# One tile of a seven-product block multiplication moved behind the next product, with its operand work reordered

## The chip, the cores and the metric

The kernel runs on one core of a Trainium2 chip. The metric is the device time of one execution in microseconds. TensorE multiplies, VectorE, ScalarE and GpSimd prepare its operands (VectorE and ScalarE also empty its result banks), and SyncE issues the transfers.

## The reference

Attention over clusters, then a layer with a squared ReLU, then the layer that matters here: four experts, each a hidden product, a ReLU and an output product, added up with each token's weight.

```python
def _moe2_ref(x, domain_probs, w1, w2):     # x 1536x512, w1 4x512x1024, w2 4x1024x512
    p = domain_probs / (domain_probs.sum(-1, keepdims=True) + 1e-09)
    out = np.zeros((N, D), dtype=np.float32)
    for e in range(E):
        h = np.maximum(x @ w1[e], 0.0)
        out += p[:, e:e + 1] * (h @ w2[e])
    return out.astype(np.float32)
```

## The kernel before

The tokens come in two batches of 768. A batch goes through 16 groups (NFQ), one for each 256 hidden columns of an expert; groups 16 to 31 are those of batch 1. All operands are split in a high and a low part, and each product is three matmuls (high x high, high x low, low x high) for each 128 of the contraction.

For batch 1 both matrix products of an expert are made in seven block products instead of eight (a Strassen-Winograd scheme: products 1 to 7, with sums of blocks as operands). `first_product(n, i)` is block product i of the hidden layer for group n: six matmuls of 384 columns. `second_product(m, i)` is block product i of the output layer for a pair of groups, a "half" of an expert, m = 0 to 7: three token tiles (j = 0, 1, 2), each six matmuls of 256 columns. The same function issues one eviction on VectorE for each tile (line 1859 or 1861), which scales the result and adds it to the output. The result banks are accumulated in turn: products 1, 6, 7 and 4 go into banks 5, 6 and 7, products 5 and 3 into banks 2, 3 and 1, and each needs that the eviction of the one before has read its bank. Product 2 uses bank 4 for tiles 0 and 2 (its two halves) and bank 0 for tile 1.

The order is written out by hand, and each engine executes its instructions in that order. The list `seq` in the loop over m interleaves the second products of half m (m1, m5, ...) with first products of later groups (3p and 4p are the rest of the group before; 1a to 4a and 1b to 7b are the two groups of half m + 2). Behind each entry, tables name operand work for half m + 1 (`SECOND`, `NEXT`; `LATE` for m = 6 and `LAST` for m = 7) or m + 2 (`SAME`); `FIRST` does so for the stretch ahead of the loop, with groups and products as keys: (17, 4) is behind product 4 of group 17. The work is named by letter and product:

- H and y make the high part of the hidden and the weight operand (ScalarE, lines 1798, 1800 and 1767);
- L and z make the low part: L on VectorE (lines 1805, 1808; a final g puts it on GpSimd), z on GpSimd (line 1770);
- S is a sum of hidden blocks on VectorE (S5 line 1785, S3 line 1788, S6 line 1794, S7 line 1792 on GpSimd with g), t a sum of weight blocks on GpSimd (line 1764);
- R is a ReLU on ScalarE (line 1781), and N a load of the next weights.

A high part comes ahead of its low part, a sum ahead of both. S5 feeds H5, t6 feeds y6. `first_product` copies product 1, 5 and 6 out with ScalarE (lines 1816, 1818, 1820), product 4 with a ReLU on ScalarE (1822), and adds products 2, 7 and 3 with VectorE (1827); product 7 accumulates on product 6's bank and so needs that product 6 was copied, product 4 likewise needs the addition of product 7.

In front of `FIRST` stands group 16 with the last token tiles of batch 0; `prep` is the weight work of group 17 (ScalarE, GpSimd).

Of the kernel before, what the change touches and what calls it, by code (L numbers as in the profile page):

```python
# [34 lines left out]
def moe_attention_kernel(  # L35
# [59 lines left out]
    NFQ = E * NQ  # L95
# [118 lines left out]
    with tc.manual_schedule():  # L214
# [808 lines left out]
        def product(n, i):  # L1023
            b, first = PROD[i][2:]
            block_product(n % 2, i, pb[n, b][:, 0:HALF], lambda x: r_op(R_OF[i], x, n // NFQ), first)
# [392 lines left out]
        def conv_in(c):  # L1418

            b = 2 * (c % 2)  # L1420
            p, q = [split64(c // 2, 0, b + m, lambda shp, m=m: cv_p[m](shp),
                            (nc.vector, nc.gpsimd)[m and c != 4]) for m in range(2)]

            def a():
                return [a_t[c // 2, 0, b + m]["a"] for m in range(2)]
            return p, q, [lambda: w_sums(a(), *([nc.vector] if c == 4 else []))], [
                [lambda m=m: w_mixed(c % 2, m, a(), nc.gpsimd)] for m in range(2)]
# [63 lines left out]
        p, q, sums2, mix = conv_in(2)  # L1491
# [9 lines left out]
        for c in range(2, NC1 - 1):  # L1501
            p, q, sums2, mix = conv_in(c + 1)
# [130 lines left out]
        def last_relu(n):  # L1633
            h_hi(n, 0, 1)
            h_lo(n, 0, 1)
            swapped(n, 3, nc.vector)
# [63 lines left out]
        def back(n, parts=KEPT):  # L1700

            if n >= 2 * NFQ:
                return
            p = (n % 2) * 1024
            for t, a, b in parts:
                for x in range(2):
                    o = 2048 * (t == "Y") + x * 1024
                    nc.sync.dma_start(
                        out=W[t][x][:, p + a * 256:p + b * 256].bitcast(F32),
                        in_=kept[n - NFQ][:, o + a * 256:o + b * 256])  # L1710
# [7 lines left out]
        def hx(m, r, q):  # L1718

            if m % 2:  # L1720
                return x2_t[r][:, q, 0:S].rearrange("p (f t) -> p f t", f=2)
            return fa8[:, ((0, 3), (2, 5))[r][q]:][:, 0:((2, 2), (5, 3))[r][q]:((1, 1), (4, 2))[r][q]]
# [12 lines left out]
        def h_op(i, x):  # L1735
            t, o = H_AT[i]
            return t[:, o + x * NR:o + (x + 1) * NR].rearrange("p (f t) -> p f t", f=2)

        def y_op(i, x):
            t, o = Y_AT[i][x]  # L1740
            return t[:, o:o + 512].rearrange("p (f d) -> p f d", f=2)
# [68 lines left out]
        def first_product(n, i):  # L1810

            m, q = divmod(n - NFQ, 2)
            product(n, i)
            a, b, c = [pb[n, z][:, 0:HALF] for z in "ABC"]
            if i == 1:
                nc.scalar.copy(hx(m, 0, q)[:, 0], a)
            elif i == 5:
                nc.scalar.copy(hx(m, 1, q)[:, 1], c)
            elif i == 6:
                nc.scalar.copy(hx(m, 1, q)[:, 0], a)  # L1820
            elif i == 4:
                nc.scalar.activation(hx(m, 0, q)[:, 1], a, AF.Relu)
                if n != NFQ + 1:
                    back(n + 2)
            else:
                o, z = {2: (hx(m, 0, q)[:, 0], b), 7: (hx(m, 1, q)[:, 1], a), 3: (hx(m, 1, q)[:, 0], c)}[i]
                nc.vector.tensor_tensor(o, z, o, op=ALU.add)  # L1827
            if n == NFQ + 1:
                back(n + 2, [W_AT[i]])

        def acc_half(t, d):
            if t < 4:
                return x2_t[t // 2][:, t % 2, S + 256 * d:S + 256 * d + 256]
            return x2_t[t - 4][:, d, S + 512:2 * S]

        BLOCK = {1: (0, 0), 5: (1, 1), 6: (0, 1), 2: (0, 0), 7: (1, 1), 3: (0, 1), 4: (1, 0)}

        def second_product(m, i):

            e = m // (NQ // 2)  # L1840
            last = m == NFQ // 2 - 1
            r, d = BLOCK[i]
            b = PROD[i][2]
            for j in range(3):
                o = {"A": bank[5 + j][:, 0:256], "C": bank[(2, 3, 1)[j]][:, 0:256],
                     "B": bank[(4, 0, 4)[j]][:, 256 * (j == 2):][:, 0:256]}[b]
                js = slice(j * 128, (j + 1) * 128)
                for f in range(2):
                    hh, hl = [h_op(i, z)[:, f, js] for z in range(2)]
                    wh, wl = [y_op(i, z)[:, f] for z in range(2)]  # L1850
                    for z, (a, w) in enumerate(((hh, wh), (hh, wl), (hl, wh))):
                        nc.tensor.matmul(  # L1852
                            o, a, w, start=(i in (1, 5, 2) and f == 0 and z == 0),
                            stop=(f == 1 and z == 2), skip_group_check=True)
                t = 3 * r + j
                pc = pe_p[:, NTT + t, e:e + 1]
                acc = acc_half(t, d)
                if m == 0 and i in (1, 5, 6, 4):
                    nc.vector.tensor_scalar(acc, o, pc, None, op0=ALU.mult)
                else:  # L1860
                    nc.vector.scalar_tensor_tensor(  # L1861
                        out=acc, in0=o, scalar=pc, in1=acc, op0=ALU.mult, op1=ALU.add)
                if last and i in (2, 7, 3, 4):
                    nc.sync.dma_start(out=ov[1, t][:, 256 * d:256 * d + 256], in_=acc)
# [7 lines left out]
        def steps(m, ws):  # L1872
            for w in ws.split():
                FS[w[0]](m, int(w[1]), *([nc.gpsimd] if w[2:] else []))

        NM = NFQ // 2
        SECOND = {"m1": "H1 y1 z1 t5 t7", "4b": "S5", "m5": "L1 H5", "m6": "S6 y5 z5 t6",
                  "m2": "H2 H6 y6 y2 z6 z2 t4", "m7": "H7", "m3": "y7 y3 z7 z3", "m4": "H4 y4 z4"}
        NEXT = {"5a": "L5", "6a": "L6", "7a": "L2", "1b": "S3", "3a": "H3 L7", "4a": "N1",
                "5b": "L3", "6b": "L4"}  # L1880
        SAME = {"7a": "R0", "6b": "R1", "2b": "S7g"}
        LATE = dict(SECOND, m2=SECOND["m2"] + " L5", m3=SECOND["m3"] + " L6", m4="H4 y4 z4 L7g")
        LAST = {"m1": "L2 S3", "m5": "H3 L3g", "m6": "L4"}
        FIRST = {(17, 1): "y5 z5 t6", (17, 5): "R1", (17, 2): "y6 y2 z6 z2 t4 S7g", (17, 4): "S5 H1 L1",
                 (18, 5): "H5 S6", (18, 6): "L5 y7 y3 H6 z7 z3", (18, 2): "L6", (18, 7): "H2 y4 z4 L2",
                 (19, 1): "S3 H7 L7g", (18, 4): "H3 H4 N1", (19, 5): "L3", (19, 6): "L4"}

        for n in range(2 * NFQ):
            pb[n, "A"] = bank[n % 2]
# [9 lines left out]
        third(NFQ - 1)  # L1899
        last_relu(NFQ - 1)  # L1900
        first_product(NFQ, 5)
        for f in prep[0:2]:
            f()
        for i in (6, 2, 7):
            first_product(NFQ, i)
        for t in range(NTT):
            token_tile(NFQ - 1, t)
# [8 lines left out]
        for n, i in [(1, 1), (1, 5), (1, 6), (1, 2), (1, 7), (2, 1), (1, 3), (1, 4), (2, 5), (2, 6), (2, 2),  # L1916
                     (2, 7), (3, 1), (2, 3), (2, 4), (3, 5), (3, 6), (3, 2), (3, 7)]:
            first_product(NFQ + n, i)
            steps(0, FIRST.get((16 + n, i), ""))
            ev = "%d%s" % (i, " ab"[n - 1])  # L1920
            if n > 1:
                steps(1, SAME.get(ev, ""))
        for m in range(NM):
            a, b = NFQ + 2 * m + 4, NFQ + 2 * m + 5
            seq = "m1 3p 4p m5 m6 m2 m7 m3 1a m4 5a 6a 2a 7a 1b 3a 4a 5b 6b 2b 7b".split()
            if m + 2 >= NM:
                seq = [x for x in seq if x[1] not in "ab" and (x[1] != "p" or m + 2 == NM)]
            for ev in seq:
                if ev[0] == "m":
                    second_product(m, int(ev[1]))  # L1930
                else:
                    first_product({"p": a - 1, "a": a, "b": b}[ev[1]], int(ev[0]))
                ev = ev.replace("p", "b") if ev in ("3p", "4p") else ev + "_" if ev in ("3b", "4b") else ev
                if m + 2 < NM:
                    steps(m + 1, SECOND.get(ev, ""))
                    steps(m + 1, NEXT.get(ev, ""))
                    steps(m + 2, SAME.get(ev, ""))
                elif m + 2 == NM:
                    steps(m + 1, LATE.get(ev, ""))
                else:  # L1940
                    steps(m, LAST.get(ev, ""))
        mctx.close()
# [30 lines left out]
```

## Time and profile before

| | us |
|---|---|
| median of 3 runs (lowest, highest) | 1016.64 (1015.82, 1018.12) |
| the profiled execution | 1016.12 |
| its span, first to last instruction | 1014.3 |
| TensorE busy in it | 991.1 (98%) |
| VectorE, ScalarE, GpSimd busy | 787.6, 576.2, 609.6 |

Matmuls are pipelined, so that busy time says only that TensorE seldom stands still. The stretch of the hidden products of batch 1 begins at about 743 us, the loop over m at 785.6, and the last matmul is issued at 1010.7.

### The profile page before, as it was taken

The page shows a single profiled execution, that of the slowest core. Times are in us where ns is not written, and L with a number is a line of the kernel's source. Part 1 is how long each engine was busy: PE and PEld are TensorE (multiplying, and loading weights), DVE is VectorE, ACT ScalarE, POOL GpSimd, SP SyncE. Part 2 cuts the span into 40 slices and gives each one's busy share as a digit, 9 for nine tenths or more (in the row PEclk, how much of TensorE's full clock was granted, in tenths as well). Part 3 has the DMA queues.
Part 4 walks back from the last instruction along what each step waited for, and adds up shares of the span by engine and source line. Part 5 has one row for each costly group of instructions (what it writes and reads, how often), then busy time and mean ns, then how long its engine had stood idle before and what let it go on. Part 6 is the DMA issues. An engine that isn't in the chain of part 4 may idle for free.

```text
span 1014.3 us, 16370 instructions
## 1 busy us (share of the span) xinstructions
PE 991.1 (98%) x5889; PEld 906.0 (89%) x5889; DVE 787.6 (78%) x1209; ACT 576.2 (57%) x1139; POOL 609.6 (60%) x589
## 2 busy tenths in 40 slices
PE   8999999999999999999999999999998999999997
PEld 8999999999888888888898998998988999999997
DVE  7898999898799997797675555577666778777786
ACT  7888888987645564445643434444445444544441
POOL 7458777753326604436666676686697654556644
PEclk9999999999999999999999999999999999999999
DMA  7577887761112212221034645545537245533411
GB/s 186 128 165 177 193 187 161 176 157 39 45 40 83 84 42 84 84 82 43 21 126 165 216 177 178 208 156 207 187 118 249 91 167 187 175 121 111 156 42 63
DMA packets 92504, 133.78 MB, mean 132 GB/s; under 512 B 29876, under 2 KB 55368, under 8 KB 92424
## 3 DMA queue, kind: packets, MB, share of 16 engines
q1 hardware_dynamic: 92424, 132.74, 43.6%
q8 instruction: 46, 0.75, 0.3%
q14 instruction: 34, 0.28, 0.1%
HBM read 80.93 MB, written 28.88 MB: 108 GB/s over the span
## 4 chain that ended last, share of the span: by engine, by line
PE 83%; DVE 7%; POOL 4%; DMA 2%; issue 2%; ACT 1%; SPq 0%; DVEq 0%; POOLq 0%; ACTq 0%
PE bank L900 23%; PE bank L931 12%; PE bank L1062 11%; PE bank L1852 8%; PE s L656 6%; PE t L689 6%; PE bank L878 5%; PE po L703 3%; PE po L705 3%; DVE x L1861 2%; DMA raw<-in_moe_w_dram 2%; DVE xa L1808 1%; PE s L878 1%; PE m L478 1%; PE m L393 1%
## 5 line engine op out<-in xcount | busy, mean ns | idle before, releaser
L695 DVE TENSOR_TENSOR ptl<-t,pth 128x384 fp32r<-128x384 f32 x192 | 98.2, 550 | 19.9 <-ACT pth L694 19.3
L900 PE MATMUL bank<-xa,wxh 128*128 128x384 f32 (+1 forms) x392 | 103.8, 345 | 0.5 <-DVE x L1827 0.5
L1861 DVE SCALAR_TENSOR_TENSOR x<-bank,pe_p,x 128x256 f32<-128x256 f32 x156 | 72.8, 480 | 35.2 <-PE bank L1852 34.4
L665 DVE TENSOR_REDUCE nb<-s 128x1 f32<-128x768 f32 x96 | 91.1, 950 | 7.9 <-PE s L656 7.5
L1078 DVE SCALAR_TENSOR_TENSOR x<-bank,pe_p,x 128x512 f32<-128x512 f32 x90 | 67.6, 751 | 35.8 <-PE bank L1062 35.7
L1006 POOL TENSOR_TENSOR wxl<-raw,wxh 128x512 fp32r<-128x512 f32 (+1 forms) x36 | 47.1, 1328 | 70.1 <-ACT wxh L1005 70.1
L694 ACT CAST pth<-t 128x384 fp32r<-128x384 f32 x192 | 84.0, 487 | 9.0 <-PE t L689 8.2
L900 PE MATMUL bank<-xa,wyh 128*128 128x384 f32 (+1 forms) x344 | 88.7, 338 | 0.0
L676 ACT ACTIVATE p<-s,nb 128x768 f32<-128x768 f32 x96 | 88.1, 918 | 0.3 <-DVE nb L665 0.2
L656 PE MATMUL s<-k,q 80*128 80x384 f32 (+1 forms) x384 | 86.2, 345 | 0.1
L689 PE MATMUL t<-identf,p 128*128 128x128 f32 x576 | 85.4, 276 | 0.4 <-DVE ptl L695 0.3
L703 PE MATMUL po<-pth,vv 128*128 128x256 f32 x288 | 80.4, 309 | 0.0
L931 PE MATMUL bank<-gb,wzh 128*128 128x512 f32 x240 | 78.0, 391 | 0.2
L689 PEld LDWEIGHTS t<-identf,p 128*128 128x128 f32 x576 | 67.6, 140 | 9.5 <-DVE ptl L695 6.8
L900 PEld LDWEIGHTS bank<-xa,wxh 128*128 128x128 f32 x392 | 71.4, 188 | 5.2 <-DVE x L1827 0.8
L900 PE MATMUL bank<-rt,wyh 128*128 128x384 f32 (+1 forms) x264 | 71.4, 351 | 3.8 <-ACT x L1820 3.4
L705 PE MATMUL po<-ptl,vv 128*128 128x256 f32 x288 | 72.5, 281 | 0.0
L900 PE MATMUL bank<-xa,wxl 128*128 128x384 f32 (+1 forms) x196 | 67.7, 345 | 0.0
L207 ACT CAST wyh<-raw 128x512 fp32r<-128x512 f32 x36 | 22.3, 622 | 78.1 <-POOL raw L200 60.7
L1770 POOL TENSOR_TENSOR wzl<-raw,wzh 128x512 fp32r<-128x512 f32 x32 | 49.9, 1562 | 26.9 <-ACT wzh L1767 26.9
L656 PEld LDWEIGHTS s<-k,q 80*128 80x128 f32 (+1 forms) x384 | 63.4, 189 | 0.6 <-ACT p L676 0.2
L900 PEld LDWEIGHTS bank<-xa,wyh 128*128 128x128 f32 x344 | 62.0, 188 | 1.4
(354 smaller groups left out, 2980.5 us busy)
## 6 DMA issues: line engine op xcount, KB each, us to landing
raw<-in_moe_w_dram SPq DMA_DIRECT2D x34, 512.0 KB, 4.6
raw<-in_moe_w_dram SPq DMA_DIRECT2D x8, 1024.0 KB, 7.6
raw<-in_moe_w_in_dram SPq DMA_DIRECT2D x7, 1024.0 KB, 5.3
kept<-wyh SPq DMA_DIRECT2D x14, 512.0 KB
kept<-wyl SPq DMA_DIRECT2D x14, 512.0 KB, 2.7
wyh<-kept SPq DMA_DIRECT2D x13, 512.0 KB, 4.6
wyl<-kept SPq DMA_DIRECT2D x13, 512.0 KB, 6.1
raw<-in_moe_w_out_dram SPq DMA_DIRECT2D x6, 1024.0 KB
```

The lines of the kernel that those rows point to most:

```text
L656: nc.tensor.matmul(s[:, j, 0:HALF], stk[i, nq][:, t * 128:(t + 1) * 128], stk[i, nk][:, j * HALF:(j + 1) * HALF], start=first, stop=not first)
L665: nc.vector.tensor_reduce(out=nb, in_=s_ps[u][:, :, 0:HALF], axis=AX.XY, op=ALU.max, negate=True)
L676: nc.scalar.activation(p, s_ps.pop(u)[:, :, 0:HALF], AF.Exp, bias=nb_t.pop(u), accum_out=sums_t[hp][:, i % 2, t:t + 1])
L689: nc.tensor.transpose(tp[:, j], p_sb[u][:, half, j * 128:(j + 1) * 128], identf)
L694: return (lambda: nc.scalar.copy(dh, tp), lambda: nc.vector.tensor_tensor(dl, tp, dh.bitcast(F32), op=ALU.subtract))
L695: lambda: nc.vector.tensor_tensor(dl, tp, dh.bitcast(F32), op=ALU.subtract))
L703: nc.tensor.matmul(po_t[pr], vt[i][:, kt], pth[:, kt], start=(kt == 0), stop=False)
L705: nc.tensor.matmul(po_t[pr], vt[i][:, kt], ptl[:, kt], start=False, stop=(kt == NTT - 1))
L900: nc.tensor.matmul(ps, w[:, ks], x(xx)[:, kt], start=(first and kt == 0 and z == 0), stop=(kt == 1 and z == 2), skip_group_check=True)
L931: nc.tensor.matmul(o, a[:, d], b, start=(ft == 0 and z == 0), stop=(ft == 1 and z == 2))
L1062: nc.tensor.matmul(o, a, w[:, f, cols], start=(f == 0 and z == 0), stop=(f == 1 and z == 2))
L1861: nc.vector.scalar_tensor_tensor(out=acc, in0=o, scalar=pc, in1=acc, op0=ALU.mult, op1=ALU.add)
```

## The change

Product 2 of the output layer is issued as two tiles (event m2) and, behind product 7, one (event m2c). The operand work is spread anew over the events: S5 goes from behind 4p to behind product 5, L1 and H5 from product 5 to product 6, S6 from product 6 to product 7; H2, y2, z2 and t4 follow the third tile, and H6 product 3. L5, L6 and L4 go one product back in the last two halves. In the stretch ahead of the loop S7 of half 0 goes from GpSimd to VectorE, H3 and L3 go to later products of group 19. In group 16, product 6 comes ahead of the weight work.

```diff
-        def second_product(m, i):
+        def second_product(m, i, js=range(3)):
...
-            for j in range(3):
+            for j in js:
...
-        SECOND = {"m1": "H1 y1 z1 t5 t7", "4b": "S5", "m5": "L1 H5", "m6": "S6 y5 z5 t6",
-                  "m2": "H2 H6 y6 y2 z6 z2 t4", "m7": "H7", "m3": "y7 y3 z7 z3", "m4": "H4 y4 z4"}
+        SECOND = {"m1": "H1 y1 z1 t5 t7", "m5": "S5", "m6": "L1 H5 y5 z5 t6", "m2": "y6 z6",
+                  "m7": "S6 H7", "m2c": "H2 y2 z2 t4", "m3": "H6 y7 y3 z7 z3", "m4": "H4 y4 z4"}
...
-        LATE = dict(SECOND, m2=SECOND["m2"] + " L5", m3=SECOND["m3"] + " L6", m4="H4 y4 z4 L7g")
-        LAST = {"m1": "L2 S3", "m5": "H3 L3g", "m6": "L4"}
-        FIRST = {(17, 1): "y5 z5 t6", (17, 5): "R1", (17, 2): "y6 y2 z6 z2 t4 S7g", (17, 4): "S5 H1 L1",
+        LATE = dict(SECOND, m3=SECOND["m3"] + " L5", m4="H4 y4 z4 L6 L7g")
+        LAST = {"m1": "L2 S3", "m5": "H3 L3g", "m7": "L4"}
+        FIRST = {(17, 1): "y5 z5 t6", (17, 5): "R1", (17, 2): "y6 y2 z6 z2 t4 S7", (17, 4): "S5 H1 L1",
                  (18, 5): "H5 S6", (18, 6): "L5 y7 y3 H6 z7 z3", (18, 2): "L6", (18, 7): "H2 y4 z4 L2",
-                 (19, 1): "S3 H7 L7g", (18, 4): "H3 H4 N1", (19, 5): "L3", (19, 6): "L4"}
+                 (19, 1): "S3 H7 L7g", (18, 4): "H4 N1", (19, 6): "H3 L4", (19, 2): "L3"}
...
         first_product(NFQ, 5)
+        first_product(NFQ, 6)
         for f in prep[0:2]:
             f()
-        for i in (6, 2, 7):
+        for i in (2, 7):
             first_product(NFQ, i)
...
-            seq = "m1 3p 4p m5 m6 m2 m7 m3 1a m4 5a 6a 2a 7a 1b 3a 4a 5b 6b 2b 7b".split()
+            seq = "m1 3p 4p m5 m6 m2 m7 m2c m3 1a m4 5a 6a 2a 7a 1b 3a 4a 5b 6b 2b 7b".split()
             if m + 2 >= NM:
-                seq = [x for x in seq if x[1] not in "ab" and (x[1] != "p" or m + 2 == NM)]
+                seq = [x for x in seq if x[-1] not in "ab" and (x[1] != "p" or m + 2 == NM)]
             for ev in seq:
                 if ev[0] == "m":
-                    second_product(m, int(ev[1]))
+                    second_product(m, int(ev[1]), {"m2": (0, 1), "m2c": (2,)}.get(ev, range(3)))
```

## Rows read from the trace of the kernel before

**Rows 1.** Waits from 745 us on: who <- for whom: us, times, longest one.
```profile
PE bank L1852 <- DVE x L1861: 10.3, 8, 2.5
```

**Rows 2.** Timeline, TensorE, m=2 and m=6: start, us, operation, count [idle before <- releaser].
```profile
854.96 3.76 PE L1852 MATMUL bank<-gb,xa 128*128 128x256 f32 x30
859.75 0.98 PE L1852 MATMUL bank<-gb,xa 128*128 128x256 f32 x6 [1.03 <-DVE x L1861]
860.57 2.32 PE L1852 MATMUL bank<-ga 128*128 128x256 f32 x18
862.72 0.28 PE L1852 MATMUL bank<-wzh,ga 128*128 128x256 f32 x1
...
984.18 0.98 PE L1852 MATMUL bank<-gb,xa 128*128 128x256 f32 x6 [1.52 <-DVE x L1861]
```

**Rows 3.** Timeline, VectorE: S5, L1, S6 in m=0; L1 and evictions in m=2.
```profile
789.71 1.70 DVE L1785 SCALAR_TENSOR_TENSOR x<-x 128x768 f32<-128x768 f32 x1
...
792.64 0.95 DVE L1808 TENSOR_TENSOR xa<-x,xa 128x768 fp32r<-128x768 f32 x1
...
794.73 2.08 DVE L1794 TENSOR_TENSOR x<-x,x 128x768 f32<-128x768 f32 x1
...
855.63 1.63 DVE L1808 TENSOR_TENSOR xa<-x,xa 128x768 fp32r<-128x768 f32 x1
...
859.22 0.86 DVE L1861 SCALAR_TENSOR_TENSOR x<-bank,pe_p,x 128x256 f32<-128x256 f32 x2
```

**Rows 4.** Timeline, three engines, the last half (m=7).
```profile
995.79 3.76 PE L1852 MATMUL bank<-gb,xa 128*128 128x256 f32 x30
...
996.47 2.57 POOL L1808 TENSOR_TENSOR ga<-raw,ga 128x768 fp32r<-128x768 f32 x1
...
997.25 2.43 DVE L1861 SCALAR_TENSOR_TENSOR x<-bank,pe_p,x 128x256 f32<-128x256 f32 x6
...
999.60 2.02 DVE L1805 SCALAR_TENSOR_TENSOR gb<-x,gb 128x768 fp32r<-128x768 f32 x1
...
1002.07 1.26 PE L1852 MATMUL bank<-gb,xa 128*128 128x256 f32 x6 [2.52 <-DVE x L1861]
...
1006.54 0.28 PE L1852 MATMUL bank<-wzh,ga 128*128 128x256 f32 x1
```

**Rows 5.** Windows: product 7 of the last half; the sixth column is TensorE's clock.
```profile
1003.13:1006.54 3.41, 3.41 (x19) 3.41 (x19) 1.45 (x3) 0.00 (x0) 0.00 (x0) 0.58 0.39 131
```

**Rows 6.** Timeline, GpSimd (z5, t6) and ScalarE (y6 y2, copies 1a, 6a), m=2.
```profile
858.37 2.06 POOL L1770 TENSOR_TENSOR wzl<-raw,wzh 128x512 fp32r<-128x512 f32 x1
860.40 1.30 POOL L1764 TENSOR_TENSOR raw<-raw 128x512 f32<-128x512 f32 x1
...
862.18 1.14 ACT L1767 CAST gb<-raw 128x512 fp32r<-128x512 f32 x2
...
866.12 0.48 ACT L1816 COPY fa<-bank 128x384 f32<-128x384 f32 x1 [0.42 <-PE bank L900]
...
870.36 0.48 ACT L1820 COPY fa<-bank 128x384 f32<-128x384 f32 x1 [0.47 <-PE bank L900]
```

**Rows 7.** Timeline ahead of the loop: waits of TensorE, VectorE and ScalarE.
```profile
749.56 0.62 PE L900 MATMUL bank<-rt,wyh 128*128 128x384 f32 x2 [0.39 <-ACT fa L1820]
...
772.44 0.96 DVE L1785 SCALAR_TENSOR_TENSOR fa<-fa 128x768 f32<-128x768 f32 x1 [3.28 <-POOL raw L1792]
773.43 0.83 ACT L1800 CAST xa<-fa 128x768 fp32r<-128x768 f32 x1 [1.93 <-DVE fa L1785]
774.69 0.62 PE L900 MATMUL bank<-rt,wyh 128*128 128x384 f32 x2 [2.04 <-ACT x L1820]
778.62 0.62 PE L900 MATMUL bank<-xa,wxh 128*128 128x384 f32 x2 [0.53 <-DVE x L1827]
782.06 0.84 ACT L1800 CAST ga<-fa 128x768 fp32r<-128x768 f32 x1 [1.57 <-DVE fa L1788]
784.43 0.62 PE L900 MATMUL bank<-rt,wyh 128*128 128x384 f32 x2 [1.35 <-ACT x L1820]
```

More of the change, by code (lines that the diff above doesn't have):

```diff
@@ L1843, in second_product @@
             b = PROD[i][2]
-            for j in range(3):
+            for j in js:
                 o = {"A": bank[5 + j][:, 0:256], "C": bank[(2, 3, 1)[j]][:, 0:256],
                      "B": bank[(4, 0, 4)[j]][:, 256 * (j == 2):][:, 0:256]}[b]
-                js = slice(j * 128, (j + 1) * 128)
+                cs = slice(j * 128, (j + 1) * 128)
                 for f in range(2):
-                    hh, hl = [h_op(i, z)[:, f, js] for z in range(2)]
+                    hh, hl = [h_op(i, z)[:, f, cs] for z in range(2)]
                     wh, wl = [y_op(i, z)[:, f] for z in range(2)]
```

## The prediction

> **What bounds the kernel now.** The waits of TensorE from 745 us on come first, because all the edited code runs there. One pair holds most of them: second_product (line 1852) waits for VectorE's evictions (line 1861) 8 times, 10.3 us in all, the longest 2.5 [rows 1]; first_product (line 900) waits twice for ScalarE's copies of product 6, 3.4 us [rows 7]. Elsewhere TensorE has its next matmul ready, so a microsecond taken out of these waits is a microsecond of the span.
>
> Then the timeline of TensorE in one half, m=2 [rows 2]. Products 6 and 2 (two of its tiles) run as 30 matmuls from 854.96; the last six matmuls of product 2, its third tile, start only at 859.75; product 7 starts at 860.57, product 3 at 862.72. Product 7 sets the pitch: 18 matmuls in 2.15 us, 0.1194 us each. Products 6, 2 and 7 are 54 matmuls, 6.45 us; they took 7.76. So the wait costs 1.31 us, 1.03 of it idle and 0.28 matmuls that restart slowly.
>
> The timeline of VectorE says why [rows 3]. By the order of the code S6 (line 1794) stands behind product 6's evictions, 2.08 us long in m=0, and only behind it come the two evictions of product 2, in m=2 from 859.22. TensorE restarts 0.05 us after the first of them has ended (859.22 + 0.48 = 859.70). Tile three lies in the other half of the bank of tile one, so it waits for that eviction.
>
> The last half is worse. There the idle is 2.52 us (L4, 2.02 us, stands ahead of the evictions) [rows 4], and the granted clock is 0.58 in the stretch behind it, a mean between its two levels (1.2 and 2.4 GHz) [rows 5]. Products 6, 2 and 7 took 1006.54 - 995.79 = 10.75 us instead of 6.45: 4.30 lost.
>
> The seven other halves have 7.8 us of idle (10.3 less 2.52) and by the pattern of m=2 seven times 0.28 more: 9.76. With the last, 14.06 us is the most that the halves can give back.
>
> **The change, part by part.**
>
> *The split of product 2.* No matmul, load, eviction or transfer is added; six matmuls and one eviction go behind product 7. The third tile is now due 24 + 24 matmuls after the start of product 6: in m=2 at 854.96 + 5.74 = 860.70. Product 7 needs the first eviction of product 6 already at 854.96 + 3.58 = 858.54.
>
> *S5, L1 and S6 on VectorE.* S5 goes behind product 5's evictions, L1 behind product 6's, S6 behind product 7's. Behind S5 wait product 6's evictions, behind L1 product 2's. Worked for m=2: product 5's last eviction ends at about 855.7, where L1 starts now [rows 3]. S5 now lies beside GpSimd's t5 and t7; so placed in m=0 it took 1.70 us [rows 3], so 857.4. The first eviction of product 6 then ends by 857.9, 0.6 before product 7 needs it. Three evictions at a pitch of 0.39 end by 858.7, L1 at its 1.63 by 860.3, tile one of product 2 is free at 860.75. Due is 860.70: the wait shrinks to nothing or 0.1. Both ends for L1: 0.95, if GpSimd is quiet (L1 in m=0), gives 0.6 of slack; 2.08, the longest of the sums (S6 in m=0) [rows 3], gives 0.5 of wait. I take 1.63, which is L1's own row beside the same GpSimd work. S6 then has all of products 2c and 3 as cover.
>
> What this L1 costs beside GpSimd is the row that decides. Of it the Trainium skill, page "SBUF — State Buffer", section "Who interferes with whom", says that a VectorE instruction with two SBUF inputs and a GpSimd instruction that reads SBUF exclude each other for a whole instruction, whoever is first. By it L1 could take 0.95 plus a full GpSimd operation of 1.30, 2.25 us, and tile three would be some 0.6 late in each half, with the restart 6.2 us over seven halves. By it the end would be at 1005.9 instead of 999.7. The rows show the slowing (1.63 and 2.08) but nothing as long as that [rows 3].
>
> *ScalarE and GpSimd.* H5 and y5 come later, since they wait for S5: y5 ends at about 857.4 + 0.83 + 0.57 = 858.8 (H5's length is that in [rows 7]), and z5 can start then. It started at 858.37 [rows 6], behind t7, so 0.4 is lost; with 2.06 and 1.30 for z5 and t6, t6 ends by 862.2. ScalarE's queue is then y6, H7, H2, y2, H6, y7, y3 and the copy of product 1a: four y at 0.57, three H at 0.83, 4.8 us, so that copy begins at 867.0 and ends at 867.5. Its reader is product 6a. Today 1a's copy begins at 866.12, when 1a ends, and 6a's at 870.36 likewise [rows 6]; 6a begins about 1.25 before that, and all is 1.31 earlier after the change: 867.8. Margin 0.3. The next reader, 7a, wants 6a's copy by about 869.9; ScalarE reaches it behind H4, y4 and 5a's copy (0.83 + 0.57 + 0.48) at 869.4 and ends at 869.85. Nothing is lost, but little is over. SP's queue keeps its order; load_second and the back transfers stand at the same products.
>
> So the six first halves (m=0 to 5) give back 9.76 less m=6's 1.80 (1.52 of idle at 984.18 [rows 2] and 0.28), 7.96 us.
>
> *The two last halves.* L6 and L4 move behind later evictions (LATE, LAST). m=6 loses its 1.80. In m=7 product 6 then starts at 995.79 - 1.80 = 993.99 and product 7 is due at 997.57. But VectorE does not come earlier: L2 and S3 are in front, and six evictions (products 5 and 6) run from 997.25 [rows 4]; the fourth, the one that product 7 waits for, ends at 997.25 + 3 x 0.39 + 0.48 = 998.9. So a new wait of 1.4 us takes the place of the one removed. L4 no longer stands in front of product 2, whose tile one is free long before 1001. L7 on GpSimd ended at 996.47 + 2.57 = 999.04 [rows 4] and is first read 0.24 behind the start of product 7: just in time. Gain of both halves 1.80 + 4.30 - 1.4 = 4.7; bounds 6.1 (no new wait) and 3.2 (VectorE or GpSimd 1.5 later).
>
> *The half's first chunk.* Four waits [rows 7]; each also restarts slowly, 0.28 as above. (18, 7) at 774.69 waits 2.04 for the copy of product 6, which ScalarE holds behind H5; H5 waits for S5, and S5 waits 3.28 us for S7 on GpSimd. With S7 on VectorE at (17, 2), S5 can start at 772.44 - 3.28 = 769.16; at 1.70 it ends by 770.9, H5 behind product 5's copy by 772.2 and the copy of 6 by 772.7, where TensorE is ready at 774.69 - 2.32 = 772.37. Gain 2.0, bounds 1.7 and 2.3. (18, 4) at 778.62 waits 0.53 for an addition at the end of a row of VectorE operations (L1, S6, L5, L6); that row starts with S5 too, as TensorE does. I take no gain; bounds 0.8 either way. (19, 7) at 784.43 waits 1.35 for product 6's copy behind H3, which waits 1.57 for S3; H3 moves behind that copy: 1.6, and only TensorE's own end holds the copy then. In the opening, product 6 goes ahead of the weight work, so its copy leaves the queue first: 0.39 + 0.28, I take 0.6. Sum 4.2.
>
> **Sum.** 7.96 + 4.7 + 4.2 = 16.9 us. The profiled execution took 1016.12, so 999.2; the median of the runs is 0.52 above it: 999.7.
>
> **The rivals.**
> - *The wait comes back behind product 7.* L1 at 2.08 instead of 1.63 makes tile three 0.4 late, and a restart costs 0.28: seven halves, 4.8 us, 1004.5. For it: the margin is about nil by my rows. Against: z5 may not yet have started when L1 runs.
> - *The end gives part of it back.* L7 or L3 on GpSimd a microsecond late in m=7, with the clock falling again as it does behind the 2.52 us (1006.54 - 1003.13 - 2.15 = 1.26 us): 2.6 us, 1002.3. For it: GpSimd has no gap there. Against: the new idle is 1.4, little over half of the one that the low clock followed.
> - *The wait does not go.* If tile three is held by a later eviction, product 7's say, the halves keep their loss and only the first chunk gains: 1012.4. Against: TensorE restarted behind one eviction of the two [rows 2, 3].
> - *Slower.* y6 waits for t6 and now stands first in ScalarE's queue, ahead of the copies that products 6a and 7a accumulate on. From 0.3 us on (for 7a almost at once), every lateness of t6 is TensorE's. It eats the 16.9 us and 2 more at 2.7 us of wait in each of seven halves, t6 3.0 late; at 3.5 late 7 x (3.2 + 0.28) = 24.4, so 1024.1. For it: the chain S5, H5, y5, z5, t6, y6 crosses three engines. Against: its slowest durations are already in the sum.
>
> **How the numbers follow.** The forecast 0.62, the returning wait 0.19, the end 0.10, no removal 0.05, slower 0.04. The likeliest is 999.7. With every wait gone it would be 14.06 + 5.43 = 19.5 us, 997.1; up to 1004.6 lie the end and most of the returning wait: 997 to 1004.6. About 2 us, 0.2%, is what a measurement here tells from nothing. All cases but the last are faster by more: 0.95, 0.02 within, 0.03 slower.
>
> **What would show it.** In the waits of TensorE, line 1852 behind line 1861 falls from 10.3 us to under 2, and what is left is in the last half, at product 7. The clock of the last half stays at 1.00. The waits of (18, 7) and (19, 7) go, that of (18, 4) stays at about 0.5. Line 900 behind ScalarE in products 6a or 7a, or one short wait per half behind line 1861, would prove me wrong.

## The result, and the profile after

The changed kernel takes 1002.27 us (median of 4 runs, 1001.82 to 1002.57) against 1016.62 for the kernel before on the same chip: a ratio of 0.9857, 95% interval 0.984 to 0.9874. The forecast was 999.7 with a range of 997.0 to 1004.6. The profiled execution took 1001.82 us, its span is 1000.0.

The waits of TensorE from 740 us on (who, for whom, us, times, longest), which answer to [rows 1]:

```profile
PE bank L900 <- DVE x L1827: 1.8, 1, 1.8
...
PE bank L1852 <- POOL ga L1808: 0.8, 1, 0.8
...
PE bank L1852 <- ACT x L1822: 0.6, 1, 0.6
PE bank L1852 <- DVE x L1861: 0.4, 1, 0.4
```

The 10.3 us of second_product behind VectorE's evictions are 0.4, and first_product no longer waits for ScalarE. Three waits are left that were not there, or were smaller. The half m=2 on the timeline, TensorE, VectorE and one row of GpSimd, answers to [rows 2, 3]:

```profile
850.22 3.76 PE L1852 MATMUL bank<-gb,xa 128*128 128x256 f32 x30
850.89 1.62 DVE L1785 SCALAR_TENSOR_TENSOR x<-x 128x768 f32<-128x768 f32 x1
...
853.61 0.94 DVE L1808 TENSOR_TENSOR xa<-x,xa 128x768 fp32r<-128x768 f32 x1
...
853.81 2.32 PE L1852 MATMUL bank<-ga 128*128 128x256 f32 x18
854.03 1.67 POOL L1770 TENSOR_TENSOR wzl<-raw,wzh 128x512 fp32r<-128x512 f32 x1 [0.36 <-ACT wzh L1767]
...
854.47 2.19 DVE L1861 SCALAR_TENSOR_TENSOR x<-bank,pe_p,x 128x256 f32<-128x256 f32 x5
...
855.97 0.88 PE L1852 MATMUL bank<-gb,xa 128*128 128x256 f32 x6
...
856.69 0.28 PE L1852 MATMUL bank<-wzh,ga 128*128 128x256 f32 x1
```

Products 6, 7 and the split product 2 now take 856.69 - 850.22 = 6.47 us; at the pitch of the prediction (0.1194 us a matmul) they are 6.45. Product 2's first eviction (854.47 + 0.48 = 854.95) is over 1.0 us before tile three starts at 855.97. The last half answers to [rows 4]:

```profile
984.13 3.76 PE L1852 MATMUL bank<-gb,xa 128*128 128x256 f32 x30
984.62 1.93 DVE L1788 SCALAR_TENSOR_TENSOR x<-x 128x768 f32<-128x768 f32 x1
986.47 3.21 DVE L1861 SCALAR_TENSOR_TENSOR x<-bank,pe_p,x 128x256 f32<-128x256 f32 x8
...
987.67 1.81 POOL L1808 TENSOR_TENSOR ga<-raw,ga 128x768 fp32r<-128x768 f32 x1
988.26 0.47 PE L1852 MATMUL bank<-ga 128*128 128x256 f32 x2 [0.37 <-DVE x L1861]
...
989.54 2.17 PE L1852 MATMUL bank<-ga 128*128 128x256 f32 x16 [0.80 <-POOL ga L1808]
...
992.27 0.28 PE L1852 MATMUL bank<-wzh,ga 128*128 128x256 f32 x1
```

Product 7 starts, runs two matmuls and stops again for the third, which reads L7 (it ends at 987.67 + 1.81 = 989.48). The whole took 992.27 - 984.13 = 8.14 us, 1.69 over the pitch, against 10.75 before. The clock stays up, in a window over product 7 (sixth column):

```profile
989.54:992.27 2.73, 2.73 (x23) 2.73 (x24) 1.64 (x5) 0.00 (x0) 1.74 (x1) 1.00 0.43 144
```

Ahead of the loop, rows of all engines that answer to [rows 7]:

```profile
769.38 1.00 DVE L1785 SCALAR_TENSOR_TENSOR fa<-fa 128x768 f32<-128x768 f32 x1
...
773.12 1.38 POOL L1770 TENSOR_TENSOR ga<-raw,ga 128x512 fp32r<-128x512 f32 x1 [1.58 <-ACT ga L1767]
773.27 2.06 DVE L1808 TENSOR_TENSOR xa<-fa,xa 128x768 fp32r<-128x768 f32 x1
775.71 1.57 DVE L1808 TENSOR_TENSOR xa<-fa,xa 128x768 fp32r<-128x768 f32 x1
777.80 0.61 PE L900 MATMUL bank<-xa,wxh 128*128 128x384 f32 x2 [1.83 <-DVE x L1827]
...
783.45 1.84 POOL L1792 TENSOR_TENSOR raw<-x,x 128x768 f32<-128x768 f32 x1 [2.51 <-ACT x L1781]
783.48 2.62 DVE L1808 TENSOR_TENSOR ga<-fa,ga 128x768 fp32r<-128x768 f32 x1
```

S5 starts at 769.38 instead of 772.44 and no longer waits for GpSimd; the 2.04 and the 1.35 us of (18, 7) and (19, 7) are gone. But (18, 4), which waited 0.53, waits 1.83.

A balance by marks on TensorE's timeline. The first product of this stretch began at 742.74 before and at 743.56 after: code that is the same in both differs by 0.82 there. From that mark to product 6 of the first half, before takes 791.97 - 742.74 = 49.23 and after 789.93 - 743.56 = 46.37: 2.86 gained, where 4.2 were forecast. From there to product 6 of the last half 203.82 and 194.20: 9.62 gained (7.96 + 1.80 = 9.76 forecast), with a new wait of 0.64 us in m=2 in it. From there to the last matmul (1010.74 and 996.47) 14.95 and 12.34: 2.61 gained, where 4.30 - 1.4 = 2.9 were forecast. Together 15.1 of 16.9; less the 0.82, the 14.3 that the spans differ by.

### The profile page after: what moved, and what is told of

It reads as the page before. It is cut to its first block, busy times and chain, and to the rows that moved or that the text cites. A ratio compares the mean times of both kernels' runs of the same rounds, so it can differ in the third digit from the quotient of the medians.

```text
span 1000.0 us, 16363 instructions
## 1 busy us (share of the span) xinstructions
PE 988.3 (99%) x5889; PEld 905.4 (91%) x5889; DVE 787.2 (79%) x1210; ACT 574.3 (57%) x1139; POOL 609.7 (61%) x588
## 4 chain that ended last, share of the span: by engine, by line
PE 90%; DVE 3%; POOL 2%; DMA 2%; ACT 1%; issue 1%; SPq 1%; POOLq 0%; ACTq 0%
PE bank L900 27%; PE bank L1062 13%; PE bank L931 13%; PE bank L1852 10%; PE s L656 6%; PE t L689 6%; PE bank L878 5%; PE po L703 3%; PE po L705 3%; PE s L878 1%; PE m L478 1%; DMA raw<-in_moe_w_dram 1%; POOL wzl L1770 1%; PE m L393 1%; PE po L1099 1%
## 5 line engine op out<-in xcount | busy, mean ns | idle before, releaser
L1861 DVE SCALAR_TENSOR_TENSOR x<-bank,pe_p,x 128x256 f32<-128x256 f32 x156 | 70.3, 478 | 27.3 <-PE bank L1852 26.2
L1770 POOL TENSOR_TENSOR wzl<-raw,wzh 128x512 fp32r<-128x512 f32 x32 | 55.2, 1736 | 31.0 <-ACT wzh L1767 31.0
```

## The experiments

Two theories. *The bank*: the halves gain because tile three no longer waits for the eviction of tile one, whose bank it shares. *The queue*: they gain because the operand work in front of product 2's evictions on VectorE was moved (S6, L1, S5), and the split matters little. The first four kernels are the one before with one edit each, on one chip (before: 1015.99 us).

**The split alone.**

```diff
-                  "m2": "H2 H6 y6 y2 z6 z2 t4", "m7": "H7", ...
+                  "m2": "H6 y6 z6", "m2c": "H2 y2 z2 t4", "m7": "H7", ...
-            seq = "... m6 m2 m7 m3 1a ..."
+            seq = "... m6 m2 m7 m2c m3 1a ..."       (m2: tiles 0 and 1, m2c: tile 2)
```

> The kernel before with the third tile of product 2 behind product 7 and nothing else (H2, y2, z2 and t4 follow that tile, as they must). Theory of the bank: six halves and m=6 give back all they give in the whole change (9.7 us); in the last half VectorE still has L4 in front of product 2's evictions, so about 1.7 of its 4.3 us comes back: 11.4 us less than before, 1005.2 us. Theory of the queue (the gain is that S6 no longer stands in front of product 2's evictions): nothing of it is undone here, so at most 2 us less than before.

1004.55 us, ratio 0.9881 (0.9866 to 0.9896): 11.4 us less, as the bank has it. The parts are not those expected: by the marks of the balance the seven halves take 195.21 us, 8.6 less than before (9.7 expected; waits of 0.2 to 0.7 us are left elsewhere in them), and from product 6 of the last half to the end it takes 11.38, 3.6 less (1.7 expected). In m=2 S6 still stands in front of product 2's evictions, and it harms nothing:

```profile
857.08 0.94 DVE L1794 TENSOR_TENSOR x<-x,x 128x768 f32<-128x768 f32 x1
857.95 2.19 DVE L1861 SCALAR_TENSOR_TENSOR x<-bank,pe_p,x 128x256 f32<-128x256 f32 x5
...
859.45 0.88 PE L1852 MATMUL bank<-gb,xa 128*128 128x256 f32 x6
```

The first eviction is over at 858.43, tile three is due a microsecond later. In the last half, where L4 still stands in front, tile three waits 0.44 us.

**The halves' new order alone**, product 2 in one piece.

```diff
-        SECOND = {... "4b": "S5", "m5": "L1 H5", "m6": "S6 y5 z5 t6", "m2": "H2 H6 y6 y2 z6 z2 t4", "m7": "H7", ...}
+        SECOND = {... "m5": "S5", "m6": "L1 H5 y5 z5 t6", "m2": "y6 z6", "m7": "S6 H7 H2 y2 z2 t4", "m3": "H6 ...", ...}
         (LATE and LAST as in the change)
```

> The kernel before with the halves' operand work in the new order (S5 behind product 5, L1 behind 6, S6 behind 7, L5, L6 and L4 one later), product 2 in one piece. Theory of the bank: L1 now stands where S6 stood, so tile three still waits about 1.0 us for tile one's eviction in seven halves; only the last half gains, since L4 is gone from the queue and its clock stays up: 3 to 4 us less than before, 1013 us. Theory of the queue: most of the halves' 12 us comes back, 1005 us.

1013.88 us, ratio 0.9974 (0.9964 to 0.9984): 2.1 less. The wait stays in all seven halves, with L1 in the place of S6 (1.02 in m=2, as before). It is 0.4 to 0.6 shorter in m=0, 3 and 6, but waits of 0.2 to 0.8 us behind ScalarE's ReLU and VectorE make up for it: by the marks of the balance the seven halves take 203.67 us against 203.82. Only the last half improves, its wait at 1.40:

```profile
860.06 0.98 PE L1852 MATMUL bank<-gb,xa 128*128 128x256 f32 x6 [1.02 <-DVE x L1861]
...
1001.37 0.98 PE L1852 MATMUL bank<-gb,xa 128*128 128x256 f32 x6 [1.40 <-DVE x L1861]
```

That ends the theory of the queue for the first seven halves.

**The stretch ahead of the loop alone** (`FIRST` and product 6 of group 16 as in the change, the halves as before).

> The kernel before with the new table ahead of the loop and product 6 of group 16 ahead of the weight work, the halves as before. If the parts add up, it takes what the traces show for this stretch, 0.6 + 2.2 us: 1013.8 us, the wait of (18, 4) at 1.8 as in the changed kernel, and the waits of the halves as before. If the halves' new order is needed for it, or it only shifts the waits into the loop, within 0.5 us of before.

1013.78 us, ratio 0.9977 (0.9967 to 0.9988): 2.2 less. The waits are those of the whole change in this stretch (1.84 us at (18, 4)) and, to 0.1, those of before in the halves, with one more of 0.57 behind line 1822 in m=2. The split alone and this edit alone sum to 13.6 us of the 14.35.

**Tile three in another bank**, the kernel before otherwise.

```diff
-                     "B": bank[(4, 0, 4)[j]][:, 256 * (j == 2):][:, 0:256]}[b]
+                     "B": bank[(4, 0, 0)[j]][:, 256 * (j == 2):][:, 0:256]}[b]
```

> The kernel before, tile three of product 2 in the free half of bank 0 (tile two's) instead of bank 4 (tile one's). Theory of the bank: it now waits for tile two's eviction, which ends 0.39 us later, in each of eight halves: 3.1 us more than before, 1019.8 us, and a wait of 1.4 in the middle halves. If the wait is for anything else on VectorE (the rest of its queue), no change.

1019.98 us, ratio 1.0042 (1.0028 to 1.0055): 4.0 more. In m=2:

```profile
859.06 0.86 DVE L1861 SCALAR_TENSOR_TENSOR x<-bank,pe_p,x 128x256 f32<-128x256 f32 x2
859.98 0.98 PE L1852 MATMUL bank<-gb,xa 128*128 128x256 f32 x6 [1.42 <-DVE x L1861]
```

TensorE starts 0.06 us after the second eviction (859.06 + 0.86) where it started 0.05 after the first [rows 3], and the wait is 0.39 longer, one eviction's pitch. In m=1 to 6 the waits grew by 0.25 to 0.40; in m=0 and the last half they shrank by 0.7, so the 4.0 us are not these waits alone: this profile has three stretches with a lowered clock (last section), that of the kernel before had one. The rest of the 4.0 is not accounted for wait by wait.

Then the waits that are left. Each of these is the changed kernel with one edit, again on one chip (before: 1016.58 us).

**L6 of half 0 later.**

```diff
-  (18, 2): "L6", (18, 7): "H2 y4 z4 L2",
+  (18, 7): "L6 H2 y4 z4 L2",
```

> The changed kernel with L6 of half 0 behind product 7 of group 18 instead of product 2 (its reader is 15 us later). If the 1.8 us wait of (18, 4) is L6 standing in VectorE's queue in front of product 7's addition (1.57 us in the trace), that wait falls to 0.3 or nothing and the time by 1.5 to 2: 1000.5 us. If the row of VectorE operations that starts with S5 sets it anyway, or the wait moves to the additions of group 19, no change.

1000.92 us, ratio 0.984 (0.9824 to 0.9857). The wait of (18, 4) falls to 0.33, and another of 1.64 turns up at product 4 of group 19, where an addition now stands behind L3:

```profile
775.42 0.62 PE L900 MATMUL bank<-xa,wxh 128*128 128x384 f32 x2 [0.33 <-DVE x L1827]
...
785.76 0.62 PE L900 MATMUL bank<-xa,wxh 128*128 128x384 f32 x2 [1.64 <-DVE x L1827]
```

So the wait moved, as in the second expectation, and the time fell, as in the first. In this profile L3 took 2.63 us. From the first mark of the balance to product 6 of the first half it took 46.37 us, as the changed kernel did, so its trace shows no gain; where the 1.5 us of the medians come from (1002.46 for the changed kernel's order on the same chip, below) is not shown. A clock that falls behind the wait of 1.8 in some executions of that order (last section) would give most of it.

**L7 of the last half earlier on GpSimd** (from behind z4, event m4, to behind H7, event m7).

> The changed kernel with L7 of the last half behind H7 (event m7) on GpSimd instead of behind z4. If L7's end holds product 7 of the last half (0.80 us idle behind GpSimd's line 1808), that wait goes and only the 0.37 behind VectorE stays: 0.9 us less, 1001.4 us. If GpSimd's total work sets the end (z2, t4, z7, z3, z4 and L3 all come 1.8 later), the wait moves to product 3 behind L3: no change.

1002.16 us, ratio 0.9855 (0.984 to 0.9869): no change. The wait behind L7 is gone, but L7 now runs beside L5, which takes 2.05 instead of 0.95, and the evictions behind it hold TensorE for 0.78 at the start of the last half:

```profile
977.41 1.86 POOL L1808 TENSOR_TENSOR ga<-raw,ga 128x768 fp32r<-128x768 f32 x1
...
978.03 2.05 DVE L1808 TENSOR_TENSOR xa<-x,xa 128x768 fp32r<-128x768 f32 x1
980.01 1.25 DVE L1861 SCALAR_TENSOR_TENSOR x<-bank,pe_p,x 128x256 f32<-128x256 f32 x3
...
980.53 0.39 PE L1852 MATMUL bank<-wzh,xa 128*128 128x256 f32 x1 [0.78 <-DVE x L1861]
```

**y1, z1, t5 and t7 behind 4p** instead of m1.

> The changed kernel with y1, z1, t5 and t7 behind product 4p instead of product m1, so that y1's wait for its transfer stands behind 4p's ReLU on ScalarE. If that order holds product 5's third tile (0.64 us idle in m=2 and smaller pieces elsewhere), the wait behind line 1822 goes: 0.9 us less, 1001.4 us. If z1, t5 and t7 come too late for y5 and y6 by it, ScalarE's copies of 1a and 6a are late and the time rises by up to 0.5 us in each half.

1001.99 us, ratio 0.9851 (0.9836 to 0.9865). No wait behind line 1822 is left, so the order on ScalarE was its cause. In time the 0.3 us to the changed kernel are too little to tell from nothing, but the trace has the gain: the seven halves take 193.20 us against 194.20 (193.19 in both kernels below that have this edit, 194.42 and 194.48 where the changed kernel's order ran again). Ahead of the loop this profile takes 1.1 us more, with a lowered clock behind the wait of (18, 4) (last section).

**z7 and z3 of half 0 later in the table.**

> The changed kernel with z7 and z3 of half 0 (GpSimd) behind product 7 of group 18 instead of product 6, L6 where it was. If the row L5, L6 is long because GpSimd works beside it (2.06 and 1.57 us against 0.95 alone), L5 takes 0.95 and L6 about 1, and the wait of (18, 4) falls from 1.8 to about 0.2: 1000.7 us. If the length is not GpSimd's doing, no change.

1002.46 us, ratio 0.9859 (0.9844 to 0.9874). The edit moved nothing: GpSimd has no other instruction between the two places, and the order on each engine is that of the changed kernel. It says nothing on its question, and is a repetition of the changed kernel on a second chip.

The last four ran on a third chip (before: 1015.69 us), the changed kernel among them.

> The changed kernel itself, as the measure for the three beside it: 1002.3 us, waits at (18, 4) of 1.8, in m=2 of 0.6 and in the last half of 0.4 and 0.8.

1002.08 us, ratio 0.9866 (0.985 to 0.9883). The waits are 1.82 at (18, 4), 0.44 in m=2, 0.37 and 0.79 in the last half.

**y7 and y3 of half 0 later on ScalarE**, so that z7 cannot start beside L5.

```diff
-  (18, 6): "L5 y7 y3 H6 z7 z3", (18, 2): "L6", (18, 7): "H2 y4 z4 L2",
+  (18, 6): "L5 H6", (18, 2): "L6", (18, 7): "y7 y3 z7 z3 H2 y4 z4 L2",
```

> The changed kernel with y7 and y3 (ScalarE), and so z7 and z3 (GpSimd), of half 0 behind product 7 of group 18; L6 stays. GpSimd then has nothing to do while L5 runs. If GpSimd's work beside it is what makes L5 2.06 us and L6 1.57, L5 takes 0.95 and the wait of (18, 4) falls from 1.8 to 0.7 or less: 1001 us. If not, L5 stays at 2 us and the time too.

999.65 us, ratio 0.9844 (0.9829 to 0.9859), 2.4 less than the changed kernel beside it. L5 and L6 take 0.95 each, and no wait of TensorE is left ahead of the loop:

```profile
773.12 0.95 DVE L1808 TENSOR_TENSOR xa<-fa,xa 128x768 fp32r<-128x768 f32 x1
...
774.46 0.95 DVE L1808 TENSOR_TENSOR xa<-fa,xa 128x768 fp32r<-128x768 f32 x1
...
774.67 1.89 POOL L1770 TENSOR_TENSOR ga<-raw,ga 128x512 fp32r<-128x512 f32 x1 [3.28 <-ACT ga L1767]
```

**L6, L3 and y1 later, together**: L6 behind (18, 7), L3 behind (19, 7), y1, z1, t5 and t7 behind 4p.

> The changed kernel with L6 of half 0 behind product 7 of group 18, L3 of half 0 behind product 7 of group 19 (so that no addition stands behind it) and y1, z1, t5 and t7 behind 4p. If the waits are those orders and nothing else, the wait of (18, 4) falls to 0.3, the wait at 4p that L6's move alone opened does not come, and the one behind line 1822 goes: 1.5 + 0.9 less, 999.9 us. If VectorE's row has simply too much work in this stretch, a wait of 1 to 2 us turns up in product 5 or 6 of half 0 instead: 1001.5 us.

1000.01 us, ratio 0.9846 (0.9832 to 0.9861). The (18, 4) wait is 0.37, line 1822 is gone, and a wait of 1.08 behind VectorE's additions is in product 5 of half 0: the second expectation in its place, the first in its time.

**The same with L7 ahead of z7.**

> The same with L7 of the last half ahead of z7 on GpSimd (event m3), behind t4, so that it no longer lies beside L5. If L7's end is the 0.8 us wait of the last half and only the company of L5 spoiled the earlier try, another 0.9 us less than that kernel: 999.0 us. If L7 beside L2 makes VectorE's evictions later instead, no change to it.

999.38 us, ratio 0.9846 (0.9831 to 0.9861), not to be told from the one above. The wait behind L7 is gone; product 7 of the last half now waits 0.83 for VectorE, whose L2 beside L7 took 2.47 us.

```profile
980.66 2.47 DVE L1805 SCALAR_TENSOR_TENSOR xa<-x,xa 128x768 fp32r<-128x768 f32 x1
...
986.81 2.39 PE L1852 MATMUL bank<-ga 128*128 128x256 f32 x18 [0.83 <-DVE x L1861]
```

Three versions are 2.1 to 2.7 us below the changed kernel beside them; the smallest edit of them is the move of y7 and y3.

## Why the prediction was right, and where it was off

*The split* was right in mechanism and size: seven halves gave 9.62 us of 9.76, and the split alone (8.6 of them), the order alone (0.15) and the other bank show that it is the shared bank. The last 1.0 us came only with both.

*S5, L1 and S6.* I put the margin of tile three at nothing, with L1 at 1.63 us beside GpSimd. It took 0.94, and the margin was 1.0 us: z5 now waits for y5, which comes with S5, and starts at 854.03, 0.42 behind L1. The argument I had written against the first rival held. S5's 1.62 and the row of evictions came out as worked. The order of the operand work was not needed in these halves (the split alone has 1.0 us of slack in m=2 with S6 in its old place), nor in the last two: from product 6 of m=6 to the end the split alone takes 27.08 us, the change 27.46, the kernel before 31.83.

*ScalarE and GpSimd.* The margins held; no wait behind ScalarE's copies turned up in any half. What I had left out is y1: its transfer kept it 2.28 us in m=2, 4p's ReLU behind it on ScalarE, and product 5's third tile for 0.64:

```profile
848.34 0.62 ACT L1767 CAST wzh<-raw 128x512 fp32r<-128x512 f32 x1 [2.28 <-DMA raw<-in_moe_w_dram]
848.87 0.48 ACT L1822 ACTIVATE x<-bank 128x384 f32<-128x384 f32 x1
...
849.40 0.39 PE L1852 MATMUL bank<-wzh,xa 128*128 128x256 f32 x1 [0.64 <-ACT x L1822]
```

That transfer takes 7.6 us from issue to landing before and after (the median of its eight on both pages of the profile), while TensorE reaches its reader earlier.

*The two last halves.* A new wait of 1.4 us at product 7 was forecast and 1.69 was measured, but of other parts. I had VectorE's row of evictions stay where it was while TensorE came 1.8 earlier; it came 0.9 earlier by itself (TensorE's product 6 moved by 995.79 - 984.13 = 11.66 us, the evictions by 997.25 - 986.47 = 10.78), and the wait for it was 0.37. L7, which I called just in time, held the third matmul for 0.80 more. That is half of the second rival, without its clock. That the sum of the end came near the forecast is luck: the wait for VectorE was 1.0 shorter than worked, and L7, with the slow restarts, filled the gap.

*The half's first chunk* is the step that failed: "I take no gain" for (18, 4), bounds 0.8 either way. It lost 1.3. I had argued that the row L1, S6, L5, L6 starts with S5, so comes earlier as TensorE does. S5 did, by 3.06 us, but L1 then waited 0.68 for H1, so that L5 came 1.90 earlier; and ScalarE's queue came earlier too, y7 with it, and z7 by 2.12. Before, L5 had started 0.07 ahead of z7:

```profile
775.17 0.95 DVE L1808 TENSOR_TENSOR xa<-fa,xa 128x768 fp32r<-128x768 f32 x1
775.24 2.05 POOL L1770 TENSOR_TENSOR ga<-raw,ga 128x512 fp32r<-128x512 f32 x1 [2.83 <-ACT ga L1767]
...
776.51 1.59 DVE L1808 TENSOR_TENSOR xa<-fa,xa 128x768 fp32r<-128x768 f32 x1
```

Now z7 started at 773.12, 0.15 ahead of L5. L5 took 2.06 where it took 0.95, and the addition of product 7 behind it came late by that 1.1 and by 0.2 more, since TensorE came 2.12 earlier and L5 only 1.90; L6, between the two, took 1.57, as before (1.59). Moving y7 away brings both to 0.95 and the wait goes: that GpSimd's work beside the two makes the wait is shown. No run lengthens or shortens L5 alone; that it is most of the 1.3 us is read from the rows. The other three waits of the stretch went as forecast.

With this goes a reading of the prediction that did not hold: that the slowing stays short of a full exclusion. L3 took 2.62 us beside S7 on GpSimd. S7 began 0.03 earlier and ended at 783.45 + 1.84 = 785.29; L3 ended 0.81 behind that, at 786.10. L5 ended at 775.33, 0.83 behind z7's 774.50. So the one that comes second does its 0.95 us nearly whole after the first. The trace before has it the other way round: behind L5 it was z7 that took 2.05. When the changed kernel ran again, L3 started 0.52 ahead of S7 and took 0.95, S7 2.13. The Trainium skill, page "SBUF — State Buffer", section "Who interferes with whom", says that a VectorE instruction with two SBUF inputs contends with GpSimd's reads, that the lock is exclusive, and that issue order decides who blocks. These rows agree, but for 0.12 to 0.14 us that the two overlap. Its warning took effect not in the halves, where I had put it, but ahead of the loop.

What stays open: the first 743 us differ by 0.8 us between the two profiles (and by up to 1.2 among all of them), in code that no edit touches. No experiment was made on it.

## What to carry to other kernels

Where two tiles of a product share a result bank, put work that needs neither between them; moving the operand work in front of the eviction only changes which operation the wait is named after. When a move pulls one engine's row earlier, ask which other queues come earlier with it: two operations on VectorE and GpSimd that started 0.07 us apart in one order can start in the other, and the one that is now second waits for the first (here 2.06 us instead of 0.95). At the end of this kernel the slack of several operands went at once, and removing one wait showed the next a microsecond behind it.

## What was not expected of the hardware

The clock does not follow the idle time alone. Before, 2.04 us of idle at 774.69 left it at 1.00; in the kernel with the other bank the same idle (2.03 us, at 775.00) was followed by 0.50, one of 1.92 us by 0.60, and one of 1.82 by 0.71 (sixth column; the first row is the kernel before):

```profile
774.69:778.00 3.31, 3.31 (x18) 3.09 (x18) 3.31 (x4) 3.31 (x7) 2.76 (x2) 1.00 0.18 69
...
775.00:776.40 1.40, 1.40 (x4) 1.40 (x5) 1.40 (x3) 1.40 (x3) 0.85 (x1) 0.50 0.40 151
...
985.92:989.00 3.08, 3.08 (x16) 3.08 (x17) 1.76 (x3) 2.02 (x4) 0.28 (x1) 0.60 0.00 0
1005.58:1009.00 3.42, 3.42 (x21) 3.42 (x22) 1.25 (x3) 0.00 (x0) 0.00 (x0) 0.71 0.40 134
```

After 1.40 us in the kernel with the new order alone, and after the 0.37 and 0.80 of the changed kernel, it stayed at 1.00. So part of what the split removed was, in the last half, a clock that a wait of 2.52 us had lowered.

One program shows both. In the profile of the changed kernel the clock stayed at 1.00 behind the 1.83 us of (18, 4); when the same kernel ran again, it was at 0.50, the lower of its two levels, behind 1.82:

```profile
777.67 0.62 PE L900 MATMUL bank<-xa,wxh 128*128 128x384 f32 x2 [1.82 <-DVE x L1827]
...
780.00:782.00 2.00, 2.00 (x8) 2.00 (x7) 2.00 (x3) 0.72 (x2) 0.79 (x1) 0.50 0.88 213
```

From the first mark of the balance to product 6 of the first half that execution took 47.49 us (47.50 and 47.51 in three more profiles with this wait and a lowered clock), the profiled one of the result 46.37, and the kernel with y7 moved 44.48. So the wait that the prediction missed costs 1.1 us more in some executions than the profile after shows. A lowered clock need not cost anything, though: before and with the new order alone the clock stayed at 1.00 behind the 2.0 us of (18, 7), with the split alone and with the other bank it fell to 0.50, and all four took 49.23 to 49.25 us over this stretch, because the later waits at (18, 4) and (19, 7), 1.9 us before, were 0.6 to 0.7 where the matmuls had been slow.
